# A gated mix of windowed attention and a token-mixing MLP: crossbar DMA transposes, w1 and w2 sharing space group by group, and operations placed by finish time

## The chip, the core and the metric

The kernel runs on one core of a Trainium2 chip. The core has five engines with instruction queues of their own: TensorE (PE, with its weight loads listed as PEld), VectorE (DVE), ScalarE (ACT), GpSimd (POOL) and SyncE (SP), which here only issues DMAs. Each engine takes its instructions in the order of the program. The metric is the device time of one execution in microseconds (us), the median of several runs.

## What is computed

```python
# x: (1, 2048, 512) bf16; S = 2048 tokens, D = 512, H = 32 heads of 16, window W = 256, F = 1376
qkv = x @ wqkv                                   # q, k, v per head
mask = (i - j >= 0) & (i - j < 256)
p = softmax(where(mask, q @ k.T * 16**-0.5, -1e9))
a = (p @ v) @ wo                                 # attention branch
h = layernorm(x)                                 # over D
u = gelu_tanh(einsum("sd,sf->df", h, w1) + b1)   # contracts over the 2048 tokens
b = (einsum("df,fs->ds", u, w2) + b2).T          # back to tokens
g = sigmoid((x * gate_w).sum(-1))
out = g * a + (1 - g) * b
```

## The kernel before, in words

**Data in SBUF.** x lies in `xo` as 16 tiles of 128 tokens, and `XT` holds its transpose (512 features on 4 x 128 partitions, 2048 tokens). Tokens are worked in four blocks of 512 (`NSB`). `wb` is one buffer that first holds w1 (16 token tiles of 1376 columns) and later w2 (11 feature tiles of 2048 columns), so that w2 can be loaded only when w1 has been used. `KT` (three blocks), `QZ` (two blocks) and `VA` hold keys, queries and values. A query tile is paired with zeros by head parity, so that one score matmul of 32 rows serves two heads.

**Stages.** Each x block is transposed by 16 PE transposes into PSUM (line 393) and two DVE copies into `XT` (line 377). The projections of a block are 12 chains of four 128x512 matmuls (helper `chain`, line 419), evicted to `KT` and `VA` by DVE or ACT (lines 376 and 377) and to `QZ` by DVE (line 459). Attention runs over 32 groups (query tile `qb`, half of the heads `hf`), each with up to three key tiles, 90 in all: eight score matmuls (line 528) into two 1024-wide PSUM pairs, two exponentials on ACT (line 547) into an `et` buffer, then a mask for the diagonal tile (DVE multiply, line 557) or for the far tile (POOL select, line 566), then 16 matmuls with the values (line 587). A reciprocal and a multiply on DVE (lines 603 and 610) give `on`. When both halves of a query tile are there, four PE transposes (line 624) and a DVE copy (line 630) write the transposed attention output over `xo`.

The MLP takes layer norm on DVE (lines 474, 478, 491, with a power on POOL, lines 484 and 485), 11 chains `u` of 16 matmuls (w1 and h), each followed by a bias on ACT (line 668), DVE and ACT steps of the gelu (lines 673 to 690), and 16 chains `y` of 11 matmuls (w2 and `ug`). Each `y` is scaled on ACT into `bp` (line 716), followed by the four matmuls of the output projection `a` (wo and `xo`), a DVE multiply-add (line 724) and an output DMA (line 729).

**What sets the order.** Every piece is a `Task` with a cost for each engine that may run it, a priority, what it depends on, and the buffers and PSUM banks that it takes. `arrange` (line 109) is a list scheduler that runs while the kernel is built: it advances a model of five engines and, at each step, puts down the task that can start first, by priority where several can. The result is the fixed order of instructions of each engine. On the chip an engine whose next instruction must wait holds everything behind it. PSUM has eight banks; `ps` gives them out in pairs for scores and singly (banks 4 to 7) for all else. The x, wqkv, w1 and wo loads are issued from SP in that order. The loads of w2 (lines 701 and 703) are tasks that depend on all of the `u` chains, with modelled landings of 2.2 + 4.5 x (1 to 4) us; the `y` chains depend on all four.

Of the kernel before, what the change touches and what calls it, by code (L numbers as in the profile page):

```python
# [8 lines left out]
BF16 = mybir.dt.bfloat16  # L9
# [99 lines left out]
def arrange(tasks, patience):  # L109
# [18 lines left out]
    while len(order) < len(tasks):  # L128
        best = None
        for e, cands in waiting.items():  # L130
            found = []
            for t in cands:
                start = max(free[e], t.ready)
                for ring, bufs in t.need.items():
                    at = ring.when(bufs)
                    if at is None:
                        start = None
                        break
                    start = max(start, at)
                if start is not None:  # L140
                    found.append((start, t))
# [31 lines left out]
    return order  # L173
@with_exitstack
def kernel(
# [27 lines left out]
    NK = 3  # L203

# [13 lines left out]
    w1 = wb[:, 0:NT * F].rearrange("p (t f) -> p t f", f=F)  # L218
    w2 = wb[:].rearrange("p (t s) -> p t s", s=S)
    ug = sb.tile([P, NFC, D], BF16, name="ug")  # L220
# [8 lines left out]
    mask = sb.tile([P, P], BF16, name="mask")  # L229
# [39 lines left out]
    ANY = (4, 5, 6, 7)  # L269

    def bank(banks=ANY):
        return ps.use(1, banks)
# [8 lines left out]

    landed = [2.3]

    def load(name, emit, kb, q="SP", deps=(), prio=0.0, small=None):
        landed[0] += kb / 370.0
        lat = small if small is not None else landed[0]
        return add(name, {q: 0.1}, emit, deps, prio, lat=lat)
# [8 lines left out]
    def load_w(name, a, z, prio):  # L296
        return load(
            name, lambda: nc.sync.dma_start(wqkv[:, :, a:z], A_wqkv[:, a:z].rearrange("(c p) n -> p c n", p=P)),
            z - a, prio=prio,
        )  # L300

    load_x(0)
    dwk = load_w("wqk", 0, 2 * D, 0.005)
    load_x(1)
    dwv = load_w("wv", 2 * D, 3 * D, 0.015)
    load_x(2)
    load_x(3)
    dw1 = []
    for i in range(4):
        def emit(i=i):  # L310
            nc.sync.dma_start(w1[:, 4 * i:4 * i + 4, :], B_w1[i * SB:(i + 1) * SB].rearrange("(t p) f -> p t f", p=P))
        dw1.append(load(f"w1_{i}", emit, 1376, prio=1 + 0.1 * i))
# [25 lines left out]
    def masks():  # L338
        nc.gpsimd.memset(b1t[:], 0.0)
        nc.gpsimd.memset(mask[:], 1.0)  # L340
        nc.gpsimd.affine_select(
            out=mask[:], in_=mask[:], pattern=[[1, P]], compare_op=ALU.is_ge, fill=0.0, base=0,
            channel_multiplier=-1,
        )

    k2 = add("masks", {"POOL": 0.8}, masks, prio=1)
# [18 lines left out]
    wu = bank()  # L365
# [7 lines left out]
    def copy_out(name, out_, in_, deps, prio, b, n, both=True):  # L373
        def emit():
            if t.engine == "ACT":
                return nc.scalar.activation(out_(), in_(), ACT.Copy)  # L376
            return nc.vector.tensor_copy(out=out_(), in_=in_())  # L377
        cost = {"DVE": n + 0.14}
        if both:
            cost["ACT"] = 0.58  # L380
        t = add(name, cost, emit, deps, prio, uses=[b])
        return t
# [3 lines left out]
    for i in range(NSB):  # L386
        for c in range(2):
            b = bank()

            def emit(i=i, c=c, b=b):  # L390
# [8 lines left out]
            t = add(f"xt{i}{c}", {"PE": 0.55}, emit, [dx[i], k1], 11 + i, takes=[b])  # L399
# [8 lines left out]
    def chain(name, mms, deps, prio, piece=2, banks=ANY):  # L408

        b = bank(banks)  # L410
# [22 lines left out]
    def project(i, prio, which):  # L433
        cols = slice(i * SB, (i + 1) * SB)
        for kind, k in which:
            if kind == "v":
                t_ = 4 * i + k
                mms = [(XT[:, ck, t_ * P:(t_ + 1) * P], wqkv[:, ck, 2 * D:3 * D], P) for ck in range(4)]
                b, t = chain(f"v{t_}", mms, [dwv, xt[i, 0], xt[i, 1], warm, k5], prio)
                vready[t_] = copy_out(  # L440
                    f"vc{t_}", lambda t_=t_: VA[:, t_, :, 0:DH],
                    lambda b=b: buf(b)[:].rearrange("p (h d) -> p h d", d=DH), [t], 4, b, 0.53,
# [7 lines left out]
            b, t = chain(f"{kind}{k}_{i}", mms, [dwk, xt[i, 0], xt[i, 1], warm] + old, prio)  # L450
            if kind == "k":
                kready[k, i] = copy_out(
                    f"kc{k}_{i}", lambda k=k: KT[:, i % NK, k, :], lambda b=b: buf(b)[:],
                    [t], 4, b, 0.53,
                )
            else:
# [6 lines left out]
                    [t, k4], 4, uses=[b],  # L463
# [5 lines left out]
    for i in range(NSB):  # L469
        ag = []  # L470
        for t_ in range(4 * i, 4 * i + 4):
# [3 lines left out]
                [dx[i]], 20 + i, takes=[b],  # L475
# [3 lines left out]
                19 + i, uses=[b],  # L479
# [8 lines left out]
        for t_ in range(4 * i, 4 * i + 4):  # L488
            hready.append(add(
                f"h{t_}", {"DVE": 0.4},  # L490
                lambda t_=t_: nc.vector.tensor_scalar(  # L491
                    out=h[:, t_, :], in0=xo[:, t_, :], scalar1=mv[:, t_, 0:1], scalar2=rstd[:, t_:t_ + 1],
                    op0=ALU.subtract, op1=ALU.mult,
                ),
                [pw], 19.5 + i,
            ))
# [9 lines left out]
    LEAD = 0.0  # L506
# [4 lines left out]
    for qb, hf in groups:  # L511
        i = qb // 4
        if qb % 4 == 0 and hf == 0 and i:
            base = {1: 21, 2: 31, 3: 41}[i]
            for n_, w in enumerate(order_k):
                project(i, base + 0.1 * n_, [w])
        kbs = [kb for kb in (qb, qb - 2, qb - 1) if kb >= 0]
        pieces = []
        for kb in kbs:
# [18 lines left out]
            s = add(f"s{qb}.{hf}.{kb}", {"PE": 0.40}, emit_s, need, 1 + 0.001 * slot, takes=b2, after=prev)  # L538
# [13 lines left out]
            prev = [(ex[0], LEAD)]  # L552
            got = ex
            if kb == qb:
                got = [add(
                    f"m{qb}.{hf}.{kb}", {"DVE": 1.15},
                    lambda e=e: nc.vector.tensor_tensor(  # L557
                        out=buf(e)[:].rearrange("p (n q) -> p n q", q=P), in0=buf(e)[:].rearrange("p (n q) -> p n q", q=P),
                        in1=mask[:, None, :].to_broadcast([P, 16, P]), op=ALU.mult,
                    ),  # L560
                    ex, 3, uses=[e],
                )]
            elif kb == qb - 2:
                got = [add(
                    f"m{qb}.{hf}.{kb}", {"POOL": 2.3},
                    lambda e=e: nc.gpsimd.affine_select(  # L566
                        out=buf(e)[:], in_=buf(e)[:], pattern=[[0, 16], [-1, P]], compare_op=ALU.is_gt, fill=0.0,
                        base=0, channel_multiplier=1,
                    ),
                    ex, 3, uses=[e],  # L570
                )]
            pieces.append((kb, e, got))
            slot += 1
        o = bank()
        last = None
        ready = [x for _, _, got in pieces for x in got]
        for n_, (kb, e, _) in enumerate(pieces):
            def emit_pv(kb=kb, e=e, n_=n_, o=o, hf=hf, total=len(pieces)):
# [15 lines left out]
                [vready[kb]] + (ready if n_ == 0 else [last]), 2 + 0.001 * slot,  # L594
# [23 lines left out]
        if len(rel[qb]) == 2:  # L618
            tb = bank()

            def emit_t(tb=tb, ob=ob):
                g16 = buf(tb)[:].bitcast(BF16)
                return [
                    nc.tensor.transpose(g16[:, c * P:(c + 1) * P], buf(ob)[:, c * P:(c + 1) * P], ident[:])  # L624
                    for c in range(4)
                ]
            tt = add(f"to{qb}", {"PE": 0.3}, emit_t, rel[qb], 8, takes=[tb], uses=[ob])
            done["ont", qb] = add(
                f"toc{qb}", {"DVE": 0.43},
                lambda tb=tb, qb=qb: nc.vector.tensor_copy(out=xo[:, qb, :], in_=buf(tb)[:].bitcast(BF16)[:, 0:D]),  # L630
                [tt, hready[qb]], 2, uses=[tb],
# [3 lines left out]
    gb = bank()  # L635
# [10 lines left out]
    gt = add("gate", {"PE": 1.8}, emit_gate, [k3] + list(xt.values()), 25, takes=[gb])  # L646
# [12 lines left out]
    for fc in range(NFC):  # L659
        f0 = fc * P  # L660
        fsz = min(P, F - f0)
        mms = [(w1[:, t_, f0:f0 + fsz], h[:, t_, :], fsz) for t_ in range(NT)]
        b, t = chain(f"u{fc}", mms, dw1 + hready, 22 + fc)
# [3 lines left out]
            f"ub{fc}", {"ACT": 0.62},  # L667
            lambda u=u, b=b, fsz=fsz, fc=fc: nc.scalar.activation(buf(u)[:fsz, :], buf(b)[:fsz, :], ACT.Identity, bias=b1c[:fsz, fc:fc + 1]),  # L668
            [t, k6], 3, takes=[u], uses=[b],
# [4 lines left out]
            [x1], 6, takes=[t1], uses=[u],  # L674
# [6 lines left out]
            [x2], 6, uses=[u, t1],  # L681
# [11 lines left out]
            [x4], 6, uses=[u, t1],  # L693
# [3 lines left out]
    edges = [0, 3, 6, 9, NFC]  # L697
    for i in range(4):
        def emit(i=i):
            a, z = edges[i], min(edges[i + 1], NFC - 1)  # L700
            nc.sync.dma_start(w2[:, a:z, :], B_w2[a * P:z * P, :].rearrange("(t p) s -> p t s", p=P))
            if i == 3:
                nc.sync.dma_start(w2[:F - (NFC - 1) * P, NFC - 1, :], B_w2[(NFC - 1) * P:F, :])
        dw2.append(add(f"w2_{i}", {"SP": 0.1}, emit, m1, 0.1 * i, lat=2.2 + 4.5 * (i + 1)))


    for qb in range(NT):
        mms = []
        for fc in range(NFC):
            fsz = min(P, F - fc * P)  # L710
            mms.append((w2[:fsz, fc, qb * P:(qb + 1) * P], ug[:fsz, fc, :], P))
        b, t = chain(f"y{qb}", mms, dw2 + ugr, 60 + qb)
        bp = bpr.use()
        yb = add(
            f"yb{qb}", {"ACT": 0.72},
            lambda bp=bp, b=b, qb=qb: nc.scalar.activation(buf(bp)[:], buf(b)[:], ACT.Identity, bias=c2[:, qb:qb + 1], scale=c1[:, qb:qb + 1]),  # L716
            [t, gd], 3, takes=[bp], uses=[b],
        )
        mms = [(xo[:, qb, c * P:(c + 1) * P], wo[:, c, :], P) for c in range(4)]
        b, t = chain(f"a{qb}", mms, [done["ont", qb], dwo, yb], 9)  # L720
# [8 lines left out]
        add(f"o{qb}", {"SP": 0.1}, lambda ot=ot, qb=qb: nc.sync.dma_start(OUT[qb * P:(qb + 1) * P, :], buf(ot)[:]), [fi], 5, uses=[ot])  # L729

    plan = arrange(tasks, 0.2)
    with tc.manual_schedule():
        last = [[] for _ in range(8)]
        for t in plan:
# [48 lines left out]
```

## Time and profile before

| | us |
|---|---|
| median of three runs (255.16 to 256.88) | 255.46 |
| the profiled execution, its own time | 255.54 |
| its span, first to last instruction | 253.7 |
| PE busy | 228.2 |
| ACT busy | 204.2 |
| DVE busy | 157.8 |
| POOL busy | 69.8 |

The mean granted TensorE clock is 0.966. In the rows of the profile, `out<-in` names what an instruction writes and reads, L12 is line 12 of the kernel, and x16 is a count. A row of a timeline joins neighbouring instructions of one group: its start, its length, its line, and in brackets the idle time before it with what ended that. Because matmuls overlap and their ends are modelled, the length of a short run of matmuls holds the latency of the last one; the distance from one row's start to the next row's start tells what the run cost.

### The profile page before, as it was taken

The page shows a single profiled execution, that of the slowest core. Times are in us where ns is not written, and L with a number is a line of the kernel's source. Part 1 is how long each engine was busy: PE and PEld are TensorE (multiplying, and loading weights), DVE is VectorE, ACT ScalarE, POOL GpSimd, SP SyncE. Part 2 cuts the span into 40 slices and gives each one's busy share as a digit, 9 for nine tenths or more (in the row PEclk, how much of TensorE's full clock was granted, in tenths as well). Part 3 has the DMA queues.
Part 4 walks back from the last instruction along what each step waited for, and adds up shares of the span by engine and source line. Part 5 has one row for each costly group of instructions (what it writes and reads, how often), then busy time and mean ns, then how long its engine had stood idle before and what let it go on. Part 6 is the DMA issues. An engine that isn't in the chain of part 4 may idle for free.

```text
span 253.7 us, 6794 instructions
## 1 busy us (share of the span) xinstructions
PE 228.2 (90%) x2968; PEld 113.3 (45%) x2968; DVE 157.8 (62%) x259; ACT 204.2 (80%) x237; POOL 69.8 (28%) x50
## 2 busy tenths in 40 slices
PE   7399988997889998998989997399999999999993
PEld 3164444643534443543434553155444555444551
DVE  4569999889998467386783888341444432435422
ACT  2028899877988988888997998997799887999921
POOL 8400230043536320332133222333333203333200
PEclk9989999999999999999999999559999999999999
DMA  6999900000000000000000199200001000101001
GB/s 233 181 374 404 357 7 4 3 4 0 3 0 3 3 0 3 3 0 3 1 3 0 28 410 407 53 3 1 23 21 44 23 21 23 41 25 43 12 33 41
DMA packets 9757, 18.00 MB, mean 71 GB/s; under 512 B 672, under 2 KB 5792, under 8 KB 9728
## 3 DMA queue, kind: packets, MB, share of 16 engines
q1 hardware_dynamic: 9568, 17.57, 19.8%
q8 instruction: 23, 0.38, 0.7%
q0 software_dynamic: 160, 0.01, 0.5%
q14 instruction: 6, 0.05, 0.1%
HBM read 15.47 MB, written 2.10 MB: 69 GB/s over the span
## 4 chain that ended last, share of the span: by engine, by line
PE 61%; ACT 16%; DVE 13%; DMA 4%; issue 4%; SPq 0%; ACTq 0%; DVEq 0%
PE pb L419 41%; ACT et L547 12%; PE pb L587 9%; PE ps L528 8%; DMA xo<-in_A_x_dram 4%; DVE h L491 2%; DVE QZ L459 2%; DVE et L557 2%; DVE t L678 1%; DVE t L673 1%; ACT uf L668 1%; PE pb L393 1%; DVE KT L377 1%; PE pb L624 1%; ACT t L685 1%
## 5 line engine op out<-in xcount | busy, mean ns | idle before, releaser
L547 ACT ACTIVATE et<-ps 128x1024 bf16<-128x1024 f32 x180 | 173.0, 1033 | 18.9 <-PE ps L528 17.6
L566 POOL TENSOR_SCALAR_AFFINE_SELECT et<-et 128x2048 bf16<-128x2048 bf16 x28 | 57.0, 2035 | 154.1 <-ACT et L547 147.2
L587 PEld LDWEIGHTS <-et 128*128 128x128 bf16 x1440 | 46.3, 96 | 23.7 <-issue 5.5
L587 PE MATMUL pb<-VA,et 128*128 128x17 bf16 x1440 | 49.9, 171 | 2.9 <-ACT et L547 1.2
L557 DVE TENSOR_TENSOR et<-et,mask 128x2048 bf16<-128x2048 bf16 x32 | 38.9, 1218 | 14.1 <-ACT et L547 13.8
L419 PE MATMUL pb<-h,wb 128*128 128x512 bf16 (+1 forms) x176 | 46.1, 380 | 1.3 <-DVE xo L630 1.3
L419 PE MATMUL pb<-ug,wb 128*128 128x512 bf16 (+1 forms) x176 | 47.1, 386 | 0.0
L528 PE MATMUL ps<-QZ,KT 32*128 32x256 bf16 x720 | 37.0, 281 | 9.8 <-ACT et L547 7.6
L419 PEld LDWEIGHTS <-wb 128*128 128x128 bf16 (+2 forms) x352 | 29.3, 99 | 33.2 <-issue 7.7
L724 DVE SCALAR_TENSOR_TENSOR ot<-pb,gg,bp 128x512 bf16<-128x512 f32 x16 | 12.0, 750 | 36.8 <-PE pb L419 19.9
L419 PE MATMUL pb<-XT,wqkv 128*128 128x512 bf16 x128 | 33.3, 385 | 1.7 <-DMA wqkv<-in_A_wqkv_dram 1.7
L528 PEld LDWEIGHTS <-KT 32*128 32x128 bf16 x720 | 10.9, 93 | 40.4 <-ACT et L547 34.2
L459 DVE TENSOR_TENSOR QZ<-pb,par 128x1024 bf16<-128x1024 f32 x16 | 19.5, 1219 | 4.1 <-PE pb L419 4.0
L419 PE MATMUL pb<-wo,xo 128*128 128x512 bf16 x64 | 18.9, 379 | 0.7 <-ACT bp L716 0.7
L419 PE MATMUL pb<-wqkv,XT 128*128 128x512 bf16 x64 | 17.2, 380 | 1.4 <-DVE VA L377 1.1
L716 ACT ACTIVATE bp<-pb,c,c 128x512 f32<-128x512 f32 x16 | 12.5, 780 | 5.8 <-PE pb L419 5.5
L419 PEld LDWEIGHTS <-wqkv 128*128 128x128 bf16 x128 | 10.6, 99 | 13.9 <-issue 1.9
L603 DVE RECIPROCAL rd<-pb 128x16 f32<-128x16 f32 x32 | 8.0, 251 | 12.7 <-PE pb L587 12.6
L376 ACT ACTIVATE KT<-pb 128x512 bf16<-128x512 f32 x6 | 3.6, 597 | 13.7 <-PE pb L419 13.6
L610 DVE TENSOR_TENSOR on<-pb,rd 128x256 bf16<-128x256 f32 x32 | 13.6, 424 | 1.1
L673 DVE TENSOR_TENSOR t<-uf 128x512 f32<-128x512 f32 (+1 forms) x11 | 9.1, 827 | 7.9 <-ACT uf L668 7.8
L690 DVE SCALAR_TENSOR_TENSOR ug<-t,uf 128x512 bf16<-128x512 f32 (+1 forms) x11 | 9.6, 873 | 3.8 <-ACT t L685 3.8
(49 smaller groups left out, 130.9 us busy)
## 6 DMA issues: line engine op xcount, KB each, us to landing
wb<-in_B_w_dram SPq DMA_DIRECT2D x4, 1376.0 KB, 15.8
wb<-in_B_w_dram SPq DMA_DIRECT2D x3, 1536.0 KB, 10.2
xo<-in_A_x_dram SPq DMA_DIRECT2D x4, 512.0 KB, 11.5
out_dram<-ot SPq DMA_DIRECT2D x16, 128.0 KB, 1.7
wqkv<-in_A_wqkv_dram SPq DMA_DIRECT2D x1, 1024.0 KB, 6.0
wqkv<-in_A_wqkv_dram SPq DMA_DIRECT2D x1, 512.0 KB, 11.8
wo<-in_A_wo_dram SPq DMA_DIRECT2D x1, 512.0 KB, 16.2
wb<-in_B_w_dram SPq DMA_DIRECT2D x1, 512.0 KB, 13.8
```

The costliest lines, as they stand in the source:

```text
L419: nc.tensor.matmul(buf(b)[:rows, :], lhsT=lhsT, rhs=rhs, start=(j == 0), stop=(j == n - 1))
L459: lambda k=k, b=b: nc.vector.tensor_tensor(out=QZ[:, i % NQ, :, k, :], in0=buf(b)[:, None, :].to_broadcast([P, 2, SB]), in1=par[:][:, :, N ...
L528: made.append(nc.tensor.matmul(buf(b2[r // 2])[:, (r % 2) * 512 + kk * 256:(r % 2) * 512 + kk * 256 + 256], lhsT=KT[32 * r:32 * r + 32, (k ...
L547: lambda j=j, b2=b2, e=e: nc.scalar.activation(out=buf(e)[:, j * 1024:(j + 1) * 1024], in_=buf(b2[j])[:], func=ACT.Exp, scale=SCALE),
L557: lambda e=e: nc.vector.tensor_tensor(out=buf(e)[:].rearrange("p (n q) -> p n q", q=P), in0=buf(e)[:].rearrange("p (n q) -> p n q", q=P), ...
L566: lambda e=e: nc.gpsimd.affine_select(out=buf(e)[:], in_=buf(e)[:], pattern=[[0, 16], [-1, P]], compare_op=ALU.is_gt, fill=0.0, base=0, ch ...
L587: made.append(nc.tensor.matmul(buf(o)[:, hl * DV:(hl + 1) * DV], lhsT=buf(e)[:, col:col + 128], rhs=VA[:, kb, head, :], start=(first and h ...
L610: lambda rd=rd, o=o, ob=ob, hf=hf: nc.vector.tensor_tensor(out=buf(ob)[:, hf * 256:(hf + 1) * 256].rearrange("p (h d) -> p h d", d=DH), in ...
L673: lambda u=u, t1=t1, fsz=fsz: nc.vector.tensor_tensor(out=buf(t1)[:fsz, :], in0=buf(u)[:fsz, :], in1=buf(u)[:fsz, :], op=ALU.mult),
L690: lambda u=u, t1=t1, fsz=fsz, fc=fc: nc.vector.scalar_tensor_tensor(out=ug[:fsz, fc, :], in0=buf(t1)[:fsz, :], scalar=1.0, in1=buf(u)[:fsz ...
L716: lambda bp=bp, b=b, qb=qb: nc.scalar.activation(buf(bp)[:], buf(b)[:], ACT.Identity, bias=c2[:, qb:qb + 1], scale=c1[:, qb:qb + 1]),
L724: lambda bp=bp, b=b, ot=ot, qb=qb: nc.vector.scalar_tensor_tensor(out=buf(ot)[:], in0=buf(b)[:], scalar=gg[:, qb:qb + 1], in1=buf(bp)[:], ...
```

## The change

- The transposes of x blocks 1 to 3 and of all 16 attention outputs become crossbar DMA transposes issued from SP. Block 0 stays on PE.
- x is loaded with four consecutive tokens to a partition ("(p t) d"), w1 likewise; wqkv is loaded as four row blocks of 1536 columns, and every projection waits for all four. The copies of block 0 into `XT` put the tokens back in order.
- `wb` is divided by groups of four feature tiles: w1's columns of group g lie exactly where w2's rows of group g will lie, w1 comes in 12 DMAs of 512 columns or 352 columns by 512 tokens, and w2's group g waits only for the `u` chains of group g.
- The scheduler takes a task on an engine only if no other engine that may run it would finish it sooner. Masks may go to DVE or POOL in both kinds, the h tiles to DVE or POOL, the evictions of `u` and `y` to ACT or DVE. Evictions get priority 60 where exponentials have 6 to 6.1.
- Priorities, PSUM banks by use, modelled costs and the modelled lead of scores over exponentials are changed.

```diff
+                end = start + t.engines[e]
+                if all(max(start, free[x]) + n >= end for x, n in t.engines.items() if x != e):
                     found.append((start, t))
...
+ORDER = dict(
+    k=52.18, q=78.76, v=68.4, u=1.2, u_step=18.14, y=84.32, a=47.23, pv=6.7, s=5.8, to=100.63, gate=229.14,
+    lead=0.63, block=67.65, xt=-11.08, patience=0.17, m=60.31, ln=98.99, ev=60.19, gelu=2.68, w1=4.9,
+)
+BANKS = dict(
+    qkv=(5, 6, 7),
+    u=(6, 7),
+    y=(4, 5),
+    a=(4, 5),
+    pv=(6, 7),
+    to=(6, 7),
+    xt=(0, 1, 2, 3, 4, 5, 6, 7),
+)
...
-    w1 = wb[:, 0:NT * F].rearrange("p (t f) -> p t f", f=F)
...
+    w1 = [
+        wb[:, 4 * S * g:4 * S * g + NT * width[g]].rearrange("p (t f) -> p t f", f=width[g]) for g in range(NG)
+    ]
...
-            nc.sync.dma_start(xo[:, 4 * i:4 * i + 4, :], X[i * SB:(i + 1) * SB].rearrange("(t p) d -> p t d", p=P))
-        dx.append(load(f"x{i}", emit, 512, prio=0.01 * len(dx)))
...
+            nc.sync.dma_start(xo[:, 4 * i:4 * i + 4, :], X[i * SB:(i + 1) * SB].rearrange("(p t) d -> p t d", t=4))
+        dx.append(load(f"x{i}", emit, 512, prio=0.01 * i))
...
+            f"wqkv{c}", lambda: nc.sync.dma_start(wqkv[:, c, :], A_wqkv[c * P:(c + 1) * P, :]), 384, prio=0.001 * (c + 1)
...
+    for g in range(NG):
+        dw1.append([])
+        for i in range(NSB):
+            def emit(i=i, g=g):
+                nc.sync.dma_start(
+                    w1[g][:, 4 * i:4 * i + 4, :],
+                    B_w1[i * SB:(i + 1) * SB, 512 * g:512 * g + width[g]].rearrange("(p t) f -> p t f", t=4),
+                )
+            dw1[g].append(load(f"w1_{g}{i}", emit, 2 * width[g], prio=ORDER["w1"] + 0.1 * g + 0.01 * i, issue=1.5))
...
+    for i in range(BYPE, NSB):
+        def emit(i=i):
+            nc.sync.dma_start_transpose(XT[:, :, i * SB:(i + 1) * SB], X[i * SB:(i + 1) * SB, :])
+        xt[i, 0] = xt[i, 1] = add(f"xt{i}", {"SP": 7.5}, emit, [], 1.05 + 0.1 * i, lat=3.0)
+    for i in range(BYPE):
...
-                lambda i=i, c=c: XT[:, 2 * c:2 * c + 2, i * SB:(i + 1) * SB],
-                lambda b=b: buf(b).bitcast(BF16).rearrange("p (c s) -> p c s", c=2),
-                [t], 5 + i, b, 0.53, both=False,
+                lambda i=i, c=c: XT[:, 2 * c:2 * c + 2, i * SB:(i + 1) * SB].rearrange("q c (p t) -> q c t p", t=4),
+                lambda b=b: buf(b).bitcast(BF16).rearrange("q (c t p) -> q c t p", c=2, t=4),
+                [t], 5 + i, b, 1.0, act=0.96,
...
+            hready.append(add(f"h{t_}", {"DVE": 0.41, "POOL": 0.75}, emit_h, [pw], ORDER["ln"] - 0.5 + i))
...
-            base = {1: 21, 2: 31, 3: 41}[i]
             for n_, w in enumerate(order_k):
-                project(i, base + 0.1 * n_, [w])
+                project(i, ORDER[w[0]] + ORDER["block"] * i + 0.01 * n_, [w])
...
-            prev = [(ex[0], LEAD)]
+            prev = [(ex[0], ORDER["lead"])]
...
+                got = [add(f"m{qb}.{hf}.{kb}", {"DVE": 1.2, "POOL": 2.1}, emit_m, ex, ORDER["m"], uses=[e])]
...
-            tt = add(f"to{qb}", {"PE": 0.3}, emit_t, rel[qb], 8, takes=[tb], uses=[ob])
             done["ont", qb] = add(
-                f"toc{qb}", {"DVE": 0.43},
-                lambda tb=tb, qb=qb: nc.vector.tensor_copy(out=xo[:, qb, :], in_=buf(tb)[:].bitcast(BF16)[:, 0:D]),
-                [tt, hready[qb]], 2, uses=[tb],
+                f"to{qb}", {"SP": 2.0},
+                lambda ob=ob, qb=qb: nc.sync.dma_start_transpose(
+                    xo[:, qb, :].rearrange("p (c q) -> p c q", c=4), buf(ob)
+                ),
+                rel[qb] + [hready[qb]], ORDER["to"], lat=2.5, uses=[ob],
             )
...
-        b, t = chain(f"u{fc}", mms, dw1 + hready, 22 + fc)
+        b, t = chain(f"u{fc}", mms, dw1[g] + hready, ORDER["u"] + ORDER["u_step"] * fc, "u")
...
-            f"ub{fc}", {"ACT": 0.62},
+            f"ub{fc}", {"ACT": 0.62, "DVE": 0.72},
...
-        dw2.append(add(f"w2_{i}", {"SP": 0.1}, emit, m1, 0.1 * i, lat=2.2 + 4.5 * (i + 1)))
+    full = NFC - 1
+    for g in range(NG):
+        def emit(g=g):
+            lo, hi = 4 * g, min(4 * g + 4, full)
+            nc.sync.dma_start(w2[:, lo:hi, :], B_w2[lo * P:hi * P, :].rearrange("(t p) s -> p t s", p=P))
+            if hi == full:
+                nc.sync.dma_start(w2[:F - full * P, full, :], B_w2[full * P:F, :])
+        dw2.append(add(f"w2_{g}", {"SP": 2.5}, emit, m1[4 * g:4 * g + 4], 0.1, lat=8.0))
...
-        b, t = chain(f"y{qb}", mms, dw2 + ugr, 60 + qb)
+        b, t = chain(f"y{qb}", mms, dw2 + ugr, ORDER["y"] + qb, "y")
...
-            f"yb{qb}", {"ACT": 0.72},
+            f"yb{qb}", {"ACT": 0.72, "DVE": 0.76},
```

More of the change, by code (lines that the diff above doesn't have):

```diff
@@ L228 @@
     ident = sb.tile([P, P], BF16, name="ident")
-    mask = sb.tile([P, P], BF16, name="mask")
+    mask = sb.tile([P, 2, P], BF16, name="mask")
     par = sb.tile([P, 2], FP32, name="par")
@@ L279, in add, with affine, load @@
         return t
+    engine = [None]
+    def affine(out_, in_, scale, bias):
+        if engine[0] == "ACT":
+            return nc.scalar.activation(out_, in_, ACT.Identity, bias=bias, scale=1.0 if scale is None else scale)
+        if scale is None:
+            return nc.vector.tensor_scalar(out=out_, in0=in_, scalar1=bias, scalar2=None, op0=ALU.add)
+        return nc.vector.tensor_scalar(out=out_, in0=in_, scalar1=scale, scalar2=bias, op0=ALU.mult, op1=ALU.add)
     landed = [2.3]
-    def load(name, emit, kb, q="SP", deps=(), prio=0.0, small=None):
+    clock = [0.0]
+    def load(name, emit, kb, q="SP", deps=(), prio=0.0, small=None, issue=0.5):
         landed[0] += kb / 370.0
+        clock[0] += issue
         lat = small if small is not None else landed[0]
-        return add(name, {q: 0.1}, emit, deps, prio, lat=lat)
+        return add(name, {q: issue}, emit, deps, prio, lat=max(2.2, lat - clock[0]))
     dx = []
@@ L340, in masks @@
         nc.gpsimd.memset(mask[:], 1.0)
[L341 to L346, printed above, removed]
+        for far in range(2):
+            nc.gpsimd.affine_select(
+                out=mask[:, far, :], in_=mask[:, far, :], pattern=[[-1 if far else 1, P]],
+                compare_op=ALU.is_gt if far else ALU.is_ge, fill=0.0, base=0, channel_multiplier=1 if far else -1,
+            )
+    k2 = add("masks", {"POOL": 1.2}, masks, prio=1)
     k3 = add("smalls", {"POOL": 4.0}, small_loads, [k2], prio=2, lat=6.0)
@@ L744 @@
                 for i in range(b.index, b.index + b.size):
-                    for engine, ins in last[i]:
-                        if engine != t.engine:
+                    for who, ins in last[i]:
+                        if who != t.engine:
                             tc.add_manual_dep(
```

157 lines of the change are left out of this document (64 added, 93 removed).

## The prediction

> **What bounds the kernel now.** I read the page's totals and clock line first, then a table of windows by stage, then the PE and ACT timelines at the places where those stand out.
>
> ```profile
> span 253.7 us, 6794 instructions
> ...
> PEclk9989999999999999999999999559999999999999
> ```
> ```profile
> 20.00:152.00 132.00, 122.94 (x1688) 60.60 (x1686) 105.39 (x169) 117.70 (x141) 35.86 (x22) 1.00 0.15 56
> ...
> 155.00:165.00 10.00, 4.12 (x95) 2.04 (x92) 5.13 (x7) 9.59 (x11) 2.34 (x2) 0.67 0.51 179
> 165.00:172.40 7.40, 7.17 (x128) 4.28 (x125) 3.06 (x7) 6.39 (x7) 3.04 (x2) 0.52 0.01 3
> 172.40:242.00 69.60, 69.13 (x878) 33.58 (x876) 27.50 (x45) 62.30 (x70) 18.80 (x10) 1.00 0.08 26
> ```
>
> The columns are the window, its length, then busy time of PE, PEld, DVE, ACT and POOL, the granted clock, DMA share and GB/s. PE is full from 20 us to the end except in one place, 155 to 165 us, where it works 4.1 of 10 us, and just behind it, to 172.4 us, it works at a clock of 0.52. ACT is nearly full as well (62.3 of 69.6 us in the long last window). So the kernel is held by PE, with ACT close behind: a gain on PE counts only as far as ACT can follow.
>
> ```profile
> 143.55 5.11 SPq L701 DMA_DIRECT2D wb<-in_B_w_dram  x4
> ```
> ```profile
> 159.17 0.61 PE L528 MATMUL ps<-QZ,KT 32*128 32x256 bf16 x8 [1.05 <-ACT et L547]
> ...
> 169.26 1.87 PE L419 MATMUL pb<-ug,wb 128*128 128x512 bf16 x4
> ```
>
> ```profile
> 55.86 0.40 PE L528 MATMUL ps<-QZ,KT 32*128 32x256 bf16 x8
> 56.19 0.56 PE L587 MATMUL pb<-VA,et 128*128 128x17 bf16 x16
> 56.61 0.59 PE L419 MATMUL pb<-wqkv,XT 128*128 128x512 bf16 x2
> ```
>
> Here all of w2 is issued only once the `u` chains release w1 (143.55 us), the projections have run out, and until the first `y` at 169.26 us PE has only scores, which wait for exponentials. The clock halves although no gap in these rows is over 1.05 us: a score group takes 0.61 us for 0.40. The last three rows give the cost of a piece at full clock, from start to start: 0.33 us for a score group, 0.42 for a value group.
>
> **The change, term by term**, against the span of 253.7 us.
>
> *w2 by groups: -8.2 us.* The idle part is 10 - 4.12 = 5.9 us. In 165 to 172.4 us, PE does 7.2 us of work; counted at full-clock distances (three score groups at 0.33, five value groups at 0.42, two transposes at 0.23, some six `y` matmuls at 0.217: about 4.9) it loses 2.3. With the change only w2's last group (1.4 MB) follows the last `u`:
>
> ```profile
> 26.00:28.00 2.00, 1.99 (x50) 1.00 1.04 410
> ```
> ```profile
> wb<-in_B_w_dram SPq DMA_DIRECT2D x3, 1536.0 KB, 10.2
> ```
>
> At 410 GB/s that is 3.5 us of data, estimated 5 to 6 us with the issue, where pieces queued behind each other took 10.2. Attention and late projections (24 chains of blocks 2 and 3, 0.87 us each) have to hide it. If that cover is gone, about 6 us at half-full PE come back: bounds -8.2 to -5.
>
> *Attention transposes off PE: -3.7 us, and -1.0 of waits.*
>
> ```profile
> 67.62 0.39 PE L624 MATMUL pb<-ident,on 128*128 128x128 bf16 x4
> 67.85 0.59 PE L419 MATMUL pb<-wqkv,XT 128*128 128x512 bf16 x2
> ```
> ```profile
> PE pb L419 <- DVE xo L630: 1.3, 2, 0.8
> ...
> PE ps L528 <- DVE xo L630: 0.7, 1, 0.7
> ```
>
> Four transposes hold the next matmul back by 0.23 us; sixteen times that is 3.7. PE also waited 2.0 us for banks that the DVE copy held; I take half, as the next wait can follow (bounds 0 to -2.0). DVE loses 16 copies of 0.42 us.
>
> *x blocks 2 and 3 off PE: -1.8 us.*
>
> ```profile
> 16.30 1.06 PE L393 MATMUL pb<-ident,xo 128*128 128x128 bf16 x16
> 17.19 0.59 PE L419 MATMUL pb<-wqkv,XT 128*128 128x512 bf16 x2
> ```
>
> Sixteen transposes of a block cost 17.19 - 16.30 = 0.89 us, two blocks 1.8.
>
> *The start: 0 us.* Block 1's transposes now hold PE until x1 has landed:
>
> ```profile
> 7.48 1.89 PE L419 MATMUL pb<-XT,wqkv 128*128 128x512 bf16 x8 [1.66 <-DMA wqkv<-in_A_wqkv_dram]
> 12.34 1.89 PE L393 MATMUL pb<-ident,xo 128*128 128x128 bf16 x16 [2.98 <-DMA xo<-in_A_x_dram]
> 14.02 2.44 PE L419 MATMUL pb<-XT,wqkv 128*128 128x512 bf16 x8
> ```
> ```profile
> 18.17 1.94 ACT L547 ACTIVATE et<-ps 128x1024 bf16<-128x1024 f32 x2 [1.50 <-PE ps L528]
> ```
> ```profile
> 6.00:7.00 1.00, 0.00 (x0) 1.00 0.96 338
> ...
> 10.00:11.00 1.00, 0.00 (x0) 1.00 1.49 137
> ```
>
> That wait goes, but the first projection, which now starts at 7.48 us, will wait for all of wqkv. x0 plus wqkv are 2.1 MB, as many bytes as x0, the first two thirds of wqkv and x1, which had landed at 12.34 us; the DMAs fall from 338 to 137 GB/s meanwhile, while the small bias loads run. Sixteen projection matmuls from 12.3 end near 14.2 + 1.6, eight from 14.02 end at 16, so the first exponential stays near 18. If the larger rows escape the slow stretch, 2.1 MB at 340 GB/s land at 8.3: bounds -4 to +1. Block 0's strided copy into `XT` lies under that wait.
>
> *DMA transposes: no row shows one.* Eight issues stand ahead of them on SP, and w1 and wo behind them. A block of 512 KB at the 410 GB/s above takes 1.3 us, the lower end. The upper end is element by element: over the first 15 us the bias loads (3,936 two-byte elements) used
>
> ```profile
> q0 software_dynamic: 160, 0.01, 8.7%
> ```
>
> which is 0.087 x 15 x 16 = 21 engine-us, or 87 us of 16 engines for the 262,144 elements of a block. The source is read in 1 KB rows like the old x load, so the nearest row is the lower one, but it is not the same operation; I take the scheduler's own entry, 7.5 us, because other new entries of the diff agree with the trace (mask 1.2 on DVE and 2.1 on POOL, against 1217 and 2005 ns here):
>
> ```profile
> L557 DVE TENSOR_TENSOR et<-et,mask x32: 1205/1217/1226, 20.6 to 236.7; 128x2048 bf16<-128x2048 bf16 x32
> L566 POOL TENSOR_SCALAR_AFFINE_SELECT et<-et x28: 1997/2005/2334, 30.2 to 239.4; 128x2048 bf16<-128x2048 bf16 x28
> ```
>
> With x3 landed near 17 us, XT1 lands near 24, XT3 near 39, and w1 by 55 (5.6 MB at 350). The rows that want them:
>
> ```profile
> 23.66 2.33 PE L419 MATMUL pb<-XT,wqkv 128*128 128x512 bf16 x10
> ...
> 51.30 1.47 PE L419 MATMUL pb<-XT,wqkv 128*128 128x512 bf16 x6
> ...
> 84.26 0.59 PE L419 MATMUL pb<-h,wb 128*128 128x512 bf16 x2
> ```
>
> are block 1 at about 24, block 2 at 51 and the first `u` at 84. So they are hidden. The smaller rows of w1 (1 KB) are hidden by the same 29 us. `to` (2.0 + 2.5 us by the entry, 32 us of SP for all sixteen, on a queue that else issues only the outputs and w2's groups by then; those stand behind it while it waits for `on`) is hidden by a `y` ahead of its `a`, except for the last query tile:
>
> ```profile
> 243.94 1.46 PE L419 MATMUL pb<-ug,wb 128*128 128x512 bf16 x6
> 245.24 0.39 PE L624 MATMUL pb<-ident,on 128*128 128x128 bf16 x4
> ...
> 247.41 0.59 PE L419 MATMUL pb<-wo,xo 128*128 128x512 bf16 x2
> ```
>
> There 2.2 us lie between the transpose and `a`, filled with `y` (six matmuls in 1.30 us, the 0.217 used above). A path of 4.5 us adds about 2 at the end: bounds 0 to +4.
>
> *Evictions, masks, h by finish time, and the new lead: -5 us.* PE idles 132 - 122.9 = 9.1 us between 20 and 152 us, in gaps behind exponentials, DVE copies and evictions. DVE is the crowded engine there (105 of 132 us) and POOL the free one (36 of 132). DVE loses 8 copies of 0.42 us, 4 XT copies, and whatever masks POOL takes at 2.0 us for 1.2. I take half of the gaps: bounds 0 to -9. The h tiles on POOL have no row; POOL's own select of four times the elements bounds one at 0.5 to 2.0 us, on an engine with the room.
>
> **The sum.** 253.7 - 8.2 - 3.7 - 1.0 - 1.8 + 0 - 5 + 2 = 236.0 us of span. The profiled execution took 255.54, 1.84 more than its span and 0.08 over the median, so 237.8: I say 238. All lower bounds together give 227 (-8.2, -3.7, -2.0, -1.8, -4, -9, 0), all upper ones 250 (-5, -3.7, 0, -1.8, +1, 0, +4): the likeliest case's own range.
>
> **Can ACT follow?**
>
> ```profile
> 237.35 4.02 ACT L547 ACTIVATE et<-ps 128x1024 bf16<-128x1024 f32 x4
> ```
> ```profile
> L716 ACT ACTIVATE bp<-pb,c,c 128x512 f32<-128x512 f32 x16 | 12.5, 780 | 5.8 <-PE pb L419 5.5
> ...
> L668 ACT ACTIVATE uf<-pb,b1c 128x512 f32<-128x512 f32 x10 | 6.9, 689 | 0.7 <-PE pb L419 0.5
> ```
>
> From 18.17 to 241.4 us ACT was busy 200 of 223, 90%. In the new span the same stretch is 18 to about 222, 204 us. At 90% 183 us fit, at 94% 192: 8 to 17 us must go to DVE, of 19 in these two rows (and 0.7 for the short chunk) and some 10 of `KT` and `VA`. DVE has 42 free us in the last window, and evictions now rank behind exponentials, so I expect that they move.
>
> **Rivals.**
>
> *ACT holds the end (0.10).* For: it is 90% busy now. Against: the two rows above may move. If none does, 200 us at 90% is 223, from 18 with 14 behind the last exponential 255.5, or 257 in all; with a third moved near 252.
>
> *Slow crossbar (0.12), the slower side.* The place is SP's queue: three x transposes ahead of w1. It decides from B, the time per block. XT1 lands at 17 + B; block 0 feeds ACT for 18 groups of two exponentials (four took 4.02 us above) from 18 us, to about 53, and block 1 needs about 15 us of shared PE before that: harmless up to B = 20. w1 lands at 17 + 3B + 16; it must stand by the order's `u`, between 45 and 84. At B = 26 w1 is there at 111 us, some 27 us after 84: the fixed order stalls PE for most of that, and 238 + 25 = 263. At B = 21 the loss is about 15 and the time 253.
>
> The Trainium skill speaks for both sides here: "VectorE: DVE Perf Modes", section "The three transpose paths", gives 1309 ns for a 128x128 crossbar transpose, an estimated B of 21 us if the 16 tiles of a block follow each other; "DMA: Bandwidth & Descriptors", section "Latency and other measured facts", gives 261 GB/s effective, an estimated B of 2. No run here shows either.
>
> *w2 still comes late (0.06).* If tracking of `wb` made its groups wait for all `u`, the 8.2 us return: 246. Against: w2's first piece was issued at 143.55, while the last `u` chain still ran:
>
> ```profile
> 148.91 0.68 ACT L668 ACTIVATE uf<-pb,b1c 96x512 f32<-96x512 f32 x1 [0.30 <-PE pb L419]
> ```
>
> *PE and ACT fit better (0.12).* All of the gaps close, the start gains 4 and the tail costs nothing: 238 - 4 - 4 - 2 = 228, and 226 if the copies' waits go too.
>
> **How the numbers follow.** The forecast has 0.60. About 1% is what a measurement of this kernel can tell. Faster by over 1% (below 252.9): 0.60 + 0.12 + 0.06 + 0.04 of ACT = 0.82. Within 1%: 0.05 of ACT and 0.02 of the crossbar, 0.07. Slower: 0.01 and 0.10, 0.11. The range runs from the better case, 226, to ACT's unmoved evictions at 256; beyond lie the slower crossbar and little else.
>
> **What would show it.** Right: no window with PE under 80% between 30 us and the last 10; the clock at 1.00 there; w2's first two groups on SP before the last `u`; SP's x transposes landing by 40 us; PE busy near 217; fewer than 22 us of evictions on ACT. Wrong: PE waiting for `XT` or `wb` by DMA, ACT without gaps to the end, or `a` waiting for `xo` by DMA query tile after query tile.

## The result and the profile after

The changed kernel takes 247.16 us (median of four runs, 246.88 to 248.11), the kernel before 255.31 us in the same comparison: a ratio of 0.9677, with a 95% interval of 0.9628 to 0.9726. It is faster, as forecast, but by 8.2 us where the forecast was 17.5. The profiled execution took 247.16 us with a span of 245.0. Where some executions of a kernel ran several us longer than its others at a lower clock, as in e4_small_late below, ratios are taken from the faster ones.

From the page of the changed kernel, the totals and the clock line:

```profile
span 245.0 us, 6531 instructions
...
PE 216.3 (88%) x2809; PEld 105.1 (43%) x2856; DVE 174.2 (71%) x266; ACT 189.7 (77%) x214; POOL 61.0 (25%) x45
...
PEclk9655999979999999999999999999999999999998
```

PE is at 216.3 us, where the prediction looked for 217, but this trace holds only 2809 of the kernel's 2856 matmuls: e12_xt1_after below, with the same order of each engine and all 2856 in its trace, shows 220.4. The two slices at half clock between 159 and 171 us of the kernel before are gone, and three at 0.5 to 0.6 stand at the start. The windows of the changed kernel (columns as before):

```profile
5.80:20.70 14.90, 0.00 (x0) 0.00 (x0) 2.45 (x3) 2.43 (x1) 2.39 (x2) 0.58 0.83 212
20.70:28.90 8.20, 8.01 (x33) 3.06 (x35) 6.29 (x14) 2.18 (x5) 5.49 (x4) 0.72 0.85 213
28.90:152.00 123.10, 117.91 (x1627) 57.31 (x1653) 105.22 (x163) 113.21 (x134) 38.06 (x21) 0.99 0.33 101
152.00:230.00 78.00, 75.08 (x1031) 37.58 (x1048) 53.56 (x73) 65.35 (x71) 10.03 (x5) 1.00 0.13 33
```

From 152 us on there is no hole any more (75.1 of 78 us). But from 5.8 to 20.7 us PE does nothing at all, and to 28.9 us it works at a clock of 0.72. The timeline of that stretch, with the SP rows of the x transposes:

```profile
5.21 10.87 SPq L427 DMA_TRANSPOSE XT<-in_A_x_dram  x1
...
18.24 2.43 ACT L419 ACTIVATE XT<-pb 128x1024 bf16<-128x1024 bf16 x1 [15.96 <-DMA XT<-in_A_x_dram]
18.25 2.42 DVE L420 COPY XT<-pb 128x1024 bf16<-128x1024 bf16 x1 [12.77 <-DMA XT<-in_A_x_dram]
...
20.73 5.85 PE L462 MATMUL pb<-XT,wqkv 128*128 128x512 bf16 x16 [14.96 <-DVE mv L521]
...
28.88 1.95 ACT L587 ACTIVATE et<-ps 128x1024 bf16<-128x1024 f32 x2
```

The two copies of block 0 from PSUM into `XT` start together at 18.2 us, and what released them is a DMA that writes `XT`: the transpose of block 1. They do not read it, and it writes other columns. PE's first projection starts when the copies end (the row names a small DVE instruction that stands next to the copy; the copy is what it needs), and the first exponential comes at 28.88 us, 10.7 us later than before. In the compiled instruction lists of both engines the copies carry a wait for the semaphore that this transpose raises, and the second x transpose one for the copies: SP holds it back for 4.6 us, until they are done.

### The profile page after: what moved, and what is told of

Same layout as the page of the kernel before. It is cut to its first block, busy times and chain, and to the rows that moved or that the text cites. A ratio compares the mean times of both kernels' runs of the same rounds, so it can differ in the third digit from the quotient of the medians.

```text
span 245.0 us, 6531 instructions
## 1 busy us (share of the span) xinstructions
PE 216.3 (88%) x2809; PEld 105.1 (43%) x2856; DVE 174.2 (71%) x266; ACT 189.7 (77%) x214; POOL 61.0 (25%) x45
## 5 line engine op out<-in xcount | busy, mean ns | idle before, releaser
L587 ACT ACTIVATE et<-ps 128x1024 bf16<-128x1024 f32 x180 | 170.7, 1039 | 19.1 <-PE ps L568 19.0
L598 DVE TENSOR_TENSOR et<-et,mask 128x2048 bf16<-128x2048 bf16 x47 | 59.0, 1255 | 14.0 <-ACT et L587 13.9
L602 POOL TENSOR_SCALAR_AFFINE_SELECT et<-et 128x2048 bf16<-128x2048 bf16 x13 | 26.1, 2008 | 125.1 <-PE pb L462 43.3
L462 PE MATMUL pb<-XT,wqkv 128*128 128x512 bf16 x120 | 35.2, 402 | 17.0 <-DVE mv L521 15.0
L462 PE MATMUL pb<-ug,wb 128*128 128x512 bf16 (+1 forms) x165 | 45.6, 380 | 1.3 <-DVE ot L754 0.4
L568 PEld LDWEIGHTS <-KT 32*128 32x128 bf16 x720 | 10.7, 92 | 33.4 <-ACT et L587 27.4
L534 POOL TENSOR_SCALAR h<-xo,mv,rstd 128x512 bf16<-128x512 bf16 x9 | 21.7, 2422 | 0.4
L754 DVE SCALAR_TENSOR_TENSOR ot<-pb,gg,bp 128x512 bf16<-128x512 f32 x16 | 12.0, 749 | 13.8 <-PE pb L462 11.7
L313 DVE TENSOR_SCALAR bp<-pb,c,c 128x512 f32<-128x512 f32 x13 | 10.5, 808 | 6.1 <-PE pb L462 6.1
L419 ACT ACTIVATE XT<-pb 128x1024 bf16<-128x1024 bf16 x1 | 2.4, 2432 | 16.0 <-DMA XT<-in_A_x_dram 16.0
L517 DVE BATCH_NORM_STATS2 stats<-xo 128x6 f32<-128x512 bf16 x16 | 10.5, 671 | 2.4 <-DMA xo<-in_A_x_dram 2.4
L720 DVE SCALAR_TENSOR_TENSOR ug<-t,uf 128x512 bf16<-128x512 f32 (+1 forms) x11 | 7.5, 685 | 6.1 <-ACT t L715 6.1
```

The costliest lines, as they stand in the source:

```text
L313: return nc.vector.tensor_scalar(out=out_, in0=in_, scalar1=scale, scalar2=bias, op0=ALU.mult, op1=ALU.add)
L462: nc.tensor.matmul(buf(b)[:rows, :], lhsT=lhsT, rhs=rhs, start=(j == 0), stop=(j == n - 1))
L517: f"bs{t_}", {"DVE": 0.67}, lambda b=b, t_=t_: nc.vector.bn_stats(buf(b)[:], xo[:, t_, :]),
L534: return eng.tensor_scalar(out=h[:, t_, :], in0=xo[:, t_, :], scalar1=mv[:, t_, 0:1], scalar2=rstd[:, t_:t_ + 1], op0=ALU.subtract, op1=AL ...
L568: made.append(nc.tensor.matmul(buf(b2[r // 2])[:, (r % 2) * 512 + kk * 256:(r % 2) * 512 + kk * 256 + 256], lhsT=KT[32 * r:32 * r + 32, (k ...
L587: lambda j=j, b2=b2, e=e: nc.scalar.activation(out=buf(e)[:, j * 1024:(j + 1) * 1024], in_=buf(b2[j])[:], func=ACT.Exp, scale=SCALE),
```

## The experiments

The theory: the loss is a wait that the data do not ask for. `XT` is one tile; block 1's DMA transpose stands ahead of the copies in the program, so the copies are made to wait for it as if they wrote the same place. Without it the forecast's sum should hold. The rival: the loads set the start, and the copies would have had to wait for wqkv anyway. Times are medians, and ratios are taken against the kernel before, run beside each. Unless said otherwise the experiments build on e1_xt_tiles.

**Tiles of their own (e1_xt_tiles).**

```diff
-    XT = sb.tile([P, 4, S], BF16, name="XT")
+    XT = [sb.tile([P, 4, SB], BF16, name=f"XT{i}") for i in range(NSB)]
...
-            nc.sync.dma_start_transpose(XT[:, :, i * SB:(i + 1) * SB], X[i * SB:(i + 1) * SB, :])
+            nc.sync.dma_start_transpose(XT[i][:], X[i * SB:(i + 1) * SB, :])
```

> The changed kernel with XT as four tiles, one for each x block, and nothing else; the order of every engine is the same. Theory (a wait that the data do not ask for): the two copies of block 0 wait for block 1's DMA transpose only because all blocks share one tile; with tiles of their own the copies start near 5.5 us in place of 18.2, the first exponential comes near 17 to 19 us in place of 28.9, and the time falls by 9 to 11 us, from 247.2 to about 237. Rival (the data set the start): wqkv itself lands late, PE still starts its projections at 16 us or later, and the time falls by less than 4 us.

Measured: 237.19 us (235.87 to 237.78), ratio 0.9261 [0.9204, 0.9319]: 10.0 us below the changed kernel. Its timeline:

```profile
4.97 2.44 ACT L419 ACTIVATE XT<-pb 128x1024 bf16<-128x1024 bf16 x1 [2.69 <-PE pb L436]
5.42 2.42 DVE L420 COPY XT<-pb 128x1024 bf16<-128x1024 bf16 x1
...
18.35 5.61 ACT L587 ACTIVATE et<-ps 128x1024 bf16<-128x1024 f32 x6
```

The copies now wait for PE's transposes alone, and the first exponential is at 18.35 us, where the prediction had put it. The rival falls.

**One tile, other program order (e12_xt1_after).** Built on the changed kernel itself.

```diff
+    plan.remove(xt[1, 0])
+    plan.insert(max(plan.index(xt[0, c]) for c in range(2)) + 1, xt[1, 0])
     with tc.manual_schedule():
```

> The changed kernel with XT as one tile again; only the program order differs: block 1's DMA transpose is put behind the two copies of block 0. The order of each engine is the same. Theory (the wait of the copies is made by the program's order of writes to one tile, not by data): the copies start near 5.5 us, the DMA transpose now waits for them until about 8 us instead, the first exponential comes at 18 to 19 us and the time is within 2 us of e1_xt_tiles, near 238. Rival (only tiles of their own remove it, or the late DMA transpose costs as much): 243 or more.

Measured: 236.64 us (235.98 to 237.25), ratio 0.9267 [0.9217, 0.9317].

```profile
5.43 2.45 ACT L419 ACTIVATE XT<-pb 128x1024 bf16<-128x1024 bf16 x1 [3.15 <-PE pb L436]
...
8.36 2.32 PE L462 MATMUL pb<-XT,wqkv 128*128 128x512 bf16 x5 [2.52 <-DVE mv L521]
...
18.45 1.95 ACT L587 ACTIVATE et<-ps 128x1024 bf16<-128x1024 f32 x2
```
```profile
8.38 12.13 SPq L427 DMA_TRANSPOSE XT<-in_A_x_dram  x3
```

Now the DMA transpose waits for the copies, to 8.38 us in place of 5.21, which costs nothing. So the order in which two writes to one tile stand in the program made the wait.

Sharing a tile does not by itself make such a wait. In this run PE reads block 0 of the same `XT` from 8.36 us on, behind block 1's DMA transpose in the program, and does not wait for it, though it took 10.0 us to land. What sets the copies apart was not run: they write block 0's columns in steps of four and across two feature tiles, with the columns of other blocks in between. Compiled with contiguous copies into the one tile, in the order of the changed kernel, the program carries neither wait, but no run shows its time.

**w2 behind all of u (e2_w2_all_u).**

```diff
-        dw2.append(add(f"w2_{g}", {"SP": 2.5}, emit, m1[4 * g:4 * g + 4], 0.1, lat=8.0))
+        dw2.append(add(f"w2_{g}", {"SP": 2.5}, emit, m1, 0.1, lat=8.0))
```

> As e1_xt_tiles, but every w2 load waits for all eleven u chains, as in the kernel before. Theory (the term of 8.2 us): PE runs out of other work and waits, with the clock reduced, and the time is 5 to 8 us above e1_xt_tiles. Rival (the scheduler finds other work for PE): under 2 us above it.

Measured: 242.70 us (242.11 to 243.74), ratio 0.9488 [0.9430, 0.9546], 5.5 us above e1_xt_tiles. The hole of the kernel before is back, smaller but with its clock, in this window:

```profile
150.00:158.00 8.00, 5.26 (x79) 2.59 (x80) 4.42 (x6) 7.80 (x9) 0.00 (x0) 0.57 0.01 2
```

PE idles 2.7 of the 8 us there. The scheduler arranged this run anew, so that the 5.5 us may hold some of its other order too.

**Output transposes back on PE (e3_to_pe).** The PE transposes and DVE copies of lines 619 to 632 of the kernel before, in place of the DMA.

> As e1_xt_tiles, but the sixteen transposes of attention outputs are on PE with a DVE copy, as in the kernel before. Theory (PE holds the end, the terms 3.7 + 1.0): 4 to 5 us above e1_xt_tiles. Rival (PE has room, ACT or DVE holds the end): under 1.5 us above it.

Measured: 252.68 us (252.61 to 254.01), ratio 0.9890 [0.9821, 0.9959]: 15.5 us above e1_xt_tiles, three times the larger of the two expectations. The scheduler had made a new order of everything, so this run does not price the transposes. The next one keeps the order.

**As many PE transposes, same order (e5_pe_extra).**

```diff
+                if first and hf == 1:
+                    g16 = buf(o)[:].bitcast(BF16)
+                    for c in range(4):
+                        made.append(nc.tensor.transpose(g16[:, 768:896], zeros[:, c * P:(c + 1) * P], ident[:]))
```

> As e1_xt_tiles with the same order of every engine, and 64 more PE transposes (four ahead of the first value group of each second half, of a constant into unused columns of that group's bank), as many as the output transposes cost PE before, with no copy and no wait of their own. Theory (PE holds the end): 64 at about 0.06 us add 3.5 to 4 us to e1_xt_tiles. Rival (PE has slack beside ACT): under 1 us; then most of the 15 us of e3_to_pe come from the scheduler's other order and not from PE's work.

Measured: 239.78 us (238.57 to 240.65), ratio 0.9405 [0.9359, 0.9450]. That is 2.6 us above e1_xt_tiles by the medians and 0.0144 x 255 = 3.7 us by the ratios. PE's work is priced nearly in full. The other 12 to 13 us of e3_to_pe are its new order together with the DVE copies and the waits for them, which e5_pe_extra leaves out; no run parts these.

**A better cost, a worse order (e9_xt_cost).**

```diff
-        xt[i, 0] = xt[i, 1] = add(f"xt{i}", {"SP": 7.5}, emit, [], 1.05 + 0.1 * i, lat=3.0)
+        xt[i, 0] = xt[i, 1] = add(f"xt{i}", {"SP": 2.0}, emit, [], 1.05 + 0.1 * i, lat=4.0)
```

> As e1_xt_tiles, but the scheduler is told the measured cost of an x transpose (2.0 us of SP and 4.0 us to landing in place of 7.5 and 3.0), and may arrange all engines anew with it. Theory (the fixed order is fragile: its priorities fit one set of modelled costs): the time changes by several us, more likely up, though the model is nearer to the chip. Rival (a better cost gives as good an order): within 2 us of e1_xt_tiles.

Measured: 254.56 us (253.02 to 256.28), ratio 0.9984 [0.9955, 1.0013]: 17 us lost by telling the scheduler the truth about one DMA. One window each, of e9_xt_cost and of e1_xt_tiles, shows where:

```profile
220.00:250.00 30.00, 16.14 (x275) 8.44 (x276) 13.90 (x19) 18.55 (x21) 0.00 (x0) 0.54 0.12 27
```
```profile
220.00:234.60 14.60, 10.41 (x95) 4.88 (x95) 4.56 (x7) 4.71 (x6) 0.00 (x0) 1.00 0.15 46
```

In the new order exponentials are left over at the end with little else for PE: ACT works 18.6 us there against 4.7, PE is half idle, and the clock is at 0.54.

**Small loads later (e4_small_late, e6_small_moved).** The first changes a dependency and lets the scheduler arrange all anew; the second moves the same loads in a fixed order.

```diff
-    k3 = add("smalls", {"POOL": 4.0}, small_loads, [k2], prio=2, lat=6.0)
+    k3 = add("smalls", {"POOL": 4.0}, small_loads, [k2, dx[3]], prio=2, lat=6.0)
```
```diff
+    hs = [t for t in plan if t.name[0] == "h" and t.engine == "POOL"]
+    plan.remove(k3)
+    plan.insert(plan.index(hs[1]) + 1, k3)
+    plan.remove(k6)
+    plan.insert(min(n for n, t in enumerate(plan) if k6 in t.deps), k6)
     with tc.manual_schedule():
```

> As e1_xt_tiles, but the four small bias and gate loads are issued only after the scheduler's time for the last x block. Theory (these loads slow the others between 7 and 12 us): DMA rates stay above 300 GB/s in that stretch, wqkv lands 2 to 4 us earlier, the first exponential too, and the time is 2 to 4 us below e1_xt_tiles. Rival (the rate falls for another reason): no change at the start, within 1 us of it.

> As e1_xt_tiles with the same order of PE, ACT and SP; only the four small loads move on POOL behind its second h tile, and the two bias casts on DVE ahead of their first use. Theory (the small loads slow the others, and the 19 us of e4_small_late came from the scheduler's other order): wqkv lands about 2 us earlier, the first exponential at about 16.5 us, the time 1 to 3 us below e1_xt_tiles. Rival (moving these loads itself does the damage): 10 us or more above it.

Measured: e4_small_late 256.00 us over all ten runs (251.14 to 259.08), ratio 0.9864 [0.9801, 0.9926] from three of them (251.14 to 253.65); e6_small_moved 234.83 us (234.54 to 235.15), ratio 0.9214 [0.9182, 0.9247]. The timeline of e6_small_moved:

```profile
8.67 5.31 PE L462 MATMUL pb<-XT,wqkv 128*128 128x512 bf16 x16 [2.52 <-DVE mv L521]
...
16.29 1.95 ACT L587 ACTIVATE et<-ps 128x1024 bf16<-128x1024 f32 x2
```

PE no longer stops for wqkv once it has started, and the first exponential is 2.1 us earlier. That is half of the 4 us which the prediction's lower bound gave the start, and it comes from taking the small loads out of the slow stretch, not from larger rows that escape it: between 10 and 12 us the DMAs move 430 and 379 GB/s, where with the small loads among them, in e1_xt_tiles, they moved 166 and 129. Moving these loads does no damage, so what e4_small_late loses, about 15 us by the ratios, is put down to its new order.

**Evictions on ACT (e8_evict_act).** In e1_xt_tiles's order, with `t.engine = "ACT"` set for every eviction of a `u` or `y` chain as it is emitted.

> As e1_xt_tiles with the same order, but all evictions of u and y chains run on ACT, as in the kernel before (some 13 of y's 16 and part of u's 11 are on DVE in e1_xt_tiles). Theory (ACT is close behind PE): some 18 evictions at 0.6 to 0.7 us bring ACT back to 200 us busy and cost 4 to 10 us. Rival (ACT has room): under 2 us.

Measured: 244.84 us (244.58 to 246.45), ratio 0.9628 [0.9577, 0.9678], 7.6 us above e1_xt_tiles. Sums of all windows, of e1_xt_tiles and of e8_evict_act:

```profile
sum 234.60, PE 216.63 PEld 105.00 DVE 173.38 ACT 189.76 POOL 60.99; mean PE 216.63 PEld 105.00 DVE 173.38 ACT 189.76 POOL 60.99
```
```profile
sum 242.90, PE 216.85 PEld 103.96 DVE 156.57 ACT 204.59 POOL 60.95; mean PE 216.85 PEld 103.96 DVE 156.57 ACT 204.59 POOL 60.95
```

ACT gets 24 more instructions (13 evictions of `y` and all 11 of `u`, where 18 were expected) and 14.8 us more work with PE's unchanged, and half of that shows in the time.

**h tiles off POOL (e10_small_h).** As e6_small_moved, with `t.engine = "DVE"` set for the h tiles as they are emitted.

> As e6_small_moved, with all h tiles on DVE at their places in the order (nine of them run on POOL there, at 2.1 us and more for the 0.75 that the scheduler assumed). Theory (POOL's h tiles only delay work that has room): within 1.5 us of e6_small_moved. Rival (they hold masks and through them PE): 2 us or more below it. A loss of 2 us or more would say that DVE is the fuller engine at that place.

Measured: 235.52 us (235.04 to 235.75), ratio 0.9218 [0.9183, 0.9253]: no difference to e6_small_moved.

**Plain copies, and the best version (e11_copy_plain).**

```diff
-X[i * SB:(i + 1) * SB].rearrange("(p t) d -> p t d", t=4))
+X[i * SB:(i + 1) * SB].rearrange("(p t) d -> p t d" if i else "(t p) d -> p t d", t=4))
...
-                lambda i=i, c=c: XT[i][:, 2 * c:2 * c + 2, :].rearrange("q c (p t) -> q c t p", t=4),
+                lambda i=i, c=c: XT[i][:, 2 * c:2 * c + 2, :],
```

> As e6_small_moved, but block 0 of x, and its rows of w1, are loaded with tokens one by one over the partitions, so that the two copies into XT are contiguous. Theory (the copy sets PE's start, since its first projection waits 2.5 us for it): the copies take under 1.1 us in place of 2.4, PE starts 1.3 us or more earlier unless wqkv is not there, and the time is 0.5 to 2 us below e6_small_moved. Rival (wqkv sets the start): no change.

Measured: 233.86 us (233.60 to 234.36), ratio 0.9157 [0.9122, 0.9193], the fastest of all. The start of its timeline:

```profile
5.37 1.02 ACT L419 ACTIVATE XT<-pb 128x1024 bf16<-128x1024 bf16 x1 [3.08 <-PE pb L436]
5.82 0.69 DVE L420 COPY XT<-pb 128x1024 bf16<-128x1024 bf16 x1 [0.25 <-PE pb L436]
...
6.57 0.39 PE L462 MATMUL pb<-XT,wqkv 128*128 128x512 bf16 x1 [0.79 <-DVE XT L420]
7.71 0.82 PE L462 MATMUL pb<-XT,wqkv 128*128 128x512 bf16 x3 [0.75 <-DMA wqkv<-in_A_wqkv_dram]
```

PE starts at 6.57 us in place of 8.67, and then wqkv holds it in turn, so that of the 2.1 us 1 us is left in the time and 0.8 us at the first exponential (15.45 us).

## Why the prediction was wrong

**The step that failed** is "The start: 0 us", with its "Block 0's strided copy into `XT` lies under that wait". The step asked when wqkv would land and took the copies to be done by then. Their real condition was block 1's DMA transpose, ahead of them in the program and on the same tile. It cost 10.0 us (247.16 against 237.19), outside the bounds of -4 to +1 given for the step; the first exponential came at 28.88 us in place of "near 18". The prediction raised just this question for `wb`, and answered it from the trace, but not for `XT`. There the trace of before could not answer it: all writes to `XT` were DVE copies, in order on one engine, so that an extra wait between them would have had no cost. The diff could have raised it: it gives one tile three kinds of writers, DMA, ACT and DVE.

**Without that wait the sum held.** e1_xt_tiles is the changed kernel without it, at 237.2 us against the 238 forecast, with the first exponential at 18.35 us against "near 18". That the total comes so near is in part luck: the terms below came out singly at other sizes, and the -1.8 of the x blocks was not tested.

**Term by term.**
- w2 by groups: -8.2 forecast, with -5 if the cover is gone. Undoing it costs 5.5 us, in an order that the scheduler made for it (e2_w2_all_u). The mechanism is the one described, down to the clock. The prediction's "no gap in these rows is over 1.05 us" holds for the rows that it shows; later score groups of that stretch wait up to 1.22 us.
- Output transposes: -3.7 and -1.0. As many transposes cost 2.6 to 3.7 us (e5_pe_extra); the copy's waits were not measured by themselves.
- The tail: +2 forecast. From the end of the last exponential to the end of the span the kernel before takes 12.3 us and e12_xt1_after 12.1, so no added time shows.
- Evictions and masks: that ACT must lose 8 to 17 us of work for PE's gain to count is borne out: it lost 14.5 (204.2 to 189.7), and giving the evictions back costs 7.6 us (e8_evict_act). PE's idle time between 20 and 152 us fell from 9.1 to 4.5 us (e12_xt1_after), about the half that the prediction took; how much of that belongs to masks, to the new lead or to priorities stays open. The h tiles on POOL were bounded too low: the first of these rows of the changed kernel gives 2422 ns in the mean (2079 at the median), over the 2.0 of the prediction, and moving them changes nothing. The second shows 13 of the 16 `y` evictions on DVE.

```profile
L534 POOL TENSOR_SCALAR h<-xo,mv,rstd 128x512 bf16<-128x512 bf16 x9 | 21.7, 2422 | 0.4
...
L313 DVE TENSOR_SCALAR bp<-pb,c,c 128x512 f32<-128x512 f32 x13 | 10.5, 808 | 6.1 <-PE pb L462 6.1
```

- The DMA transposes: the prediction took 7.5 us for a block while it called a plain load the nearest row. The changed kernel's SP rows and landing times:

```profile
L427 SPq DMA_TRANSPOSE XT<-in_A_x_dram x3: 1876/1952/10872, 5.2 to 22.7; - x3
...
L657 SPq DMA_TRANSPOSE xo<-on x16: 1188/1191/1625, 57.3 to 236.3; - x16
```
```profile
XT<-in_A_x_dram SPq DMA_TRANSPOSE x3, 4.1
```

An issue takes 1.9 us for a 512x512 block and 1.2 us for an output tile (the 10.9 us are the first one, issued with all loads still ahead of it), and the two later blocks land 4.1 us after. 512 KB at the 1.95 us from one issue to the next are an estimated 269 GB/s; in e1_xt_tiles the two later issues took 2.0 and 2.4 us. Of the two pages of the Trainium skill weighed in the prediction, "DMA: Bandwidth & Descriptors", section "Latency and other measured facts", is near this with its 261 GB/s. The 1309 ns that the Trainium skill gives for a 128x128 tile in "VectorE: DVE Perf Modes", section "The three transpose paths", do not describe tiles that follow each other: 16 of them took 1.95 us here. The slow crossbar is out as a rival; the slower side was never near.

**Of the signs named beforehand**, "SP's x transposes landing by 40 us" (the last at 26.8), fewer than 22 us of evictions on ACT (11.7), no window of 10 us with PE under 80%, and w2's first two groups ahead of the last `u`, which ran to 149 us, came out right (the issues of the two groups in the changed kernel):

```profile
100.17 0.39 SPq L731 DMA_DIRECT2D wb<-in_B_w_dram  x1
...
128.57 0.37 SPq L731 DMA_DIRECT2D wb<-in_B_w_dram  x1
```

PE busy was 3 us above 217 when all matmuls are in the trace (220.4), and the clock was not 1.00 throughout: 0.96 from 40 to 50 us and 0.87 from 50 to 60. The sign for "wrong", PE waiting for `XT`, is what appeared, though one step removed: copies waited for the DMA and PE for the copies.

## What to carry to other kernels

When a change moves one of several writers of a tile to another engine or to a DMA, list for each write which earlier writes of the same tile stand ahead of it in the program, and look in the trace or the instruction list for a wait between them that the data do not ask for; where there is one, give parts of their own to writers that need not wait for each other, or put the early one first. An order planned from modelled costs is to be compared with the order held fixed: one entry corrected cost 17 us here, more than any single part of the change brought. And a cost taken from a scheduler's table is not a measurement, even where its neighbours agree with the trace.

## What the runs showed of the hardware

A copy of 128x1024 bf16 from PSUM into four interleaved token groups took 2.42 us on DVE and 2.43 to 2.45 on ACT (the changed kernel, e1_xt_tiles, e12_xt1_after), and 0.69 and 1.02 us where it was contiguous (e11_copy_plain). The clock was 0.57 in the window of e2_w2_all_u shown above, with gaps of 0.5 to 1.1 us between score groups and PE busy for 5.3 of 8 us. In the changed kernel POOL took 2.1 us at the median for an h tile of 512 columns (subtract and multiply by two columns of scalars), about as long as for a select of 2048 columns (2.0 us). Four small loads of 3,936 two-byte elements in all held the DMAs at 166 and 129 GB/s between 10 and 12 us (e1_xt_tiles), against 430 and 379 with these loads moved (e6_small_moved).
